# Whole F32 products for the first 256 tokens, and weights split after them, in a fused attention and expert kernel

## The chip, the cores and the metric

The kernel runs on one core of one Trainium2 chip. The metric is the device time of one execution in microseconds; of several executions the median is quoted. TensorE (PE) multiplies matrices, VectorE (DVE), ScalarE (ACT) and GpSimd (POOL) work elementwise, and SyncE (SP) issues the transfers. Each engine runs its own instructions in the order in which the program lists them and waits for others by semaphores.

## What is computed

Three layers stand in a row, over 4 sequences of 768 tokens with 8 heads of 48 columns (3072 tokens, 384 columns in all). The first is an attention with a complex decay per token and column (`a_re`, `a_im`, scaled to a magnitude of at most 0.999), the second an expert layer with a rational activation, the third a layer that changes only tokens whose score is positive.

```python
for t in range(S):
    ar, ai = (a_re_n[:, :, t, :, None], a_im_n[:, :, t, :, None])
    new_re = ar * S_re - ai * S_im
    new_im = ar * S_im + ai * S_re
    kv = np.einsum('bhd,bhe->bhde', k[:, :, t], v[:, :, t])
    S_re, S_im = (new_re + kv, new_im)
    y[:, :, t] = np.einsum('bhd,bhde->bhe', q[:, :, t], S_re)
...
x = np.ascontiguousarray(attn_out.transpose(0, 2, 1, 3)).reshape(B * S, H * D)
...
h = x @ w_in
h2 = h * h
h3 = h2 * h
P = a[0] + a[1] * h + a[2] * h2 + a[3] * h3
Q = 1.0 + np.abs(b[0]) * np.abs(h) + np.abs(b[1]) * h2
g = P / (Q + 1e-06)
return (g @ w_out).astype(np.float32)
...
do_compute = skip_score > 0
out = x.copy()
```

`w_in` is 384 x 2048 and `w_out` 2048 x 384; both arrive as 64-bit floats.

## The kernel before

**Tiling.** The 3072 tokens are worked through in 12 units of 256 (`u`), each of two chunks of 128. Of a unit, the attention part (`early`, `trig`, `cums`, `prods`, `chunk`) turns decays into sums of logarithms and angles, takes exponentials and sines, and makes scores and states by small products; `yevac` brings the result to SBUF and splits it into a rounded part `xh` and the rest `xl`. The expert part is 8 steps per unit (`step`, 96 in all). A step has two halves of G1 (line 819: 128 hidden columns x 256 tokens, three products of 384 input rows each), ten elementwise operations on a 128 x 512 tile (lines 366, 805 on ScalarE, 809 on VectorE), the split of their result into `gh` and `gl` (lines 848 and 851, GpSimd), and two halves of G2 (line 865), which add into the two `ob` banks.

**Split products.** The kernel multiplies in the type F32R. Each F32 operand stands as a rounded high part and the rest, the low part, and a product is three: high times high, high times low, low times high. Half a step of G1 is thus 9 matrix instructions of 256 columns and half a step of G2 is 6 of 384.

**Weights.** `weight_in` (8 transfers of 768 KB) and `weight_out` (16 of 384 KB) load the 64-bit words, and `weight` unpacks a piece of 384 columns by three VectorE operations (lines 395, 398, 405) and one scaling on ScalarE or GpSimd (366, 402), then rounds it on ScalarE (413) and subtracts on GpSimd (417). There are 32 such pieces. For room they unpack in buffers that have another use later: `weight_in` in `wk`, whose parts are the steps' `u` (`ub`) and `qa` (`qab`), `weight_out` in `xh1`, `xl1`, `x2b`, the last two parts of `wk`, `gh` and `gl`. Steps are listed behind all weights, and so a step's first elementwise operation, which writes `u` or `qa`, waits until all eight loads of `weight_in` have been unpacked and split.

**Order.** All work is listed as tasks in a `Plan`, with engines that may do it, a cost on each and what it reads and writes. `order` plays the list through by these costs: each engine takes the ready task with the lowest rank. A rank is a due time (`start`, `due`) or is counted back from the tasks that follow; `PP` holds the numbers that shape it. On TensorE a task in the other mode (`cols`: scores, values and updates of the state, which use parts of the array) is put back by `AF`. The result is written out in that order for every engine. Where the play leaves TensorE a gap between 5 us and `start(NP) + X1`, `filled` puts in products without a reader (lines 942, 946, 949); line 310 clears the banks at the start.

**After the steps** the output tiles are scaled, stored and scored (lines 366, 878, 883), and `flags` decides whether the rare paths run; they don't here.

## Time and profile before

| | us |
|---|---|
| median of 3 runs (653.58 to 654.98) | 653.9 |
| the profiled execution | 654.03 |
| its span, first to last instruction | 652.2 |
| mean share of the full TensorE clock granted | 0.994 |
| TensorE busy | 632.7 |
| ScalarE busy | 564.9 |
| VectorE busy | 534.3 |
| GpSimd busy | 426.5 |

The profile is of one execution; its span is 1.8 us shorter than the time that this execution took. "Busy" is time in which an engine works on at least one instruction; products overlap, so their durations add up to more than TensorE's busy time. A table by stretch gives for each engine the busy time inside it and the instructions in brackets, then the granted TensorE clock, the share of the time that the transfer engines are busy, and GB/s. A group of instructions is told by line, engine, operation and tiles, with its count, busy time and the mean duration of one in ns; behind the second bar stands the idle time before them. The view of one line gives minimum, median and maximum in ns and the first and last start. In the views by time a row gives start, duration and the instructions merged in it.

### The profile page before, as it was taken

How to read it: one execution, taken by the hardware profiler on the slowest of the kernel's cores; microseconds unless marked ns; L12 is line 12 of the kernel's file. 1: busy time of each engine (PE TensorE's matmuls, PEld its weight loads, DVE VectorE, ACT ScalarE, POOL GpSimd, SP SyncE). 2: the span in 40 equal slices, each digit the busy share in tenths (PEclk: the TensorE clock that was granted, in tenths of full speed). 3: DMA queues.
4: the chain of work that ended last, by engine and by line, in shares of the span. 5: the costliest groups of instructions: out<-in, count | busy, mean ns of one | idle time of the engine just before them, and what ended most of it. 6: DMA issues, size and time to landing. Idle time of an engine off the chain costs nothing.

```text
span 652.2 us, 15284 instructions
## 1 busy us (share of the span) xinstructions
PE 632.7 (97%) x5852; PEld 604.6 (93%) x5852; DVE 534.3 (82%) x859; ACT 564.9 (87%) x938; POOL 426.5 (65%) x425
## 2 busy tenths in 40 slices
PE   7899899999999999999999999999999999999994
PEld 6798889999999999999999999999999999999994
DVE  5999999898878798798798798798798797675772
ACT  6888899998999998997999997998999996976771
POOL 6688968876586686665576676665676766634442
PEclk9989999999999999999999999999999999999998
DMA  8728514113103023023112023023013020010000
GB/s 326 219 86 265 167 47 119 50 48 95 51 22 100 28 62 101 5 60 93 33 47 78 24 66 102 1 65 95 25 47 101 2 66 4 4 45 5 25 1 30
DMA packets 43698, 45.81 MB, mean 70 GB/s; under 512 B 19680, under 2 KB 40544, under 8 KB 43616
## 3 DMA queue, kind: packets, MB, share of 16 engines
q1 hardware_dynamic: 43616, 44.74, 22.7%
q8 instruction: 48, 0.79, 0.5%
q14 instruction: 34, 0.28, 0.1%
HBM read 38.73 MB, written 4.72 MB: 67 GB/s over the span
## 4 chain that ended last, share of the span: by engine, by line
PE 84%; DVE 6%; POOL 4%; ACT 2%; issue 1%; DMA 1%; SPq 0%; POOLq 0%; DVEq 0%
PE ob L865 30%; PE zb L819 30%; PE zb L671 6%; PE zb L691 5%; PE zb L714 4%; PE zb L737 3%; PE zb L716 2%; PE ob L949 2%; POOL kt L369 1%; DMA ar<-in_a_re_dram 1%; DVE zb L398 1%; DVE zb L395 1%; PE zb L593 1%; PE zb L620 1%; POOL gl L851 1%
## 5 line engine op out<-in xcount | busy, mean ns | idle before, releaser
L809 DVE SCALAR_TENSOR_TENSOR wk<-wk,cf,zb 128x512 f32<-128x512 f32 x192 | 141.8, 743 | 57.1 <-ACT zb L805 42.7
L819 PE MATMUL zb<-xh,wih 128*128 128x256 f32 x576 | 165.9, 288 | 0.2 <-DVE pT L696 0.2
L819 PE MATMUL zb<-xl,wih 128*128 128x256 f32 x576 | 162.3, 282 | 0.0
L819 PE MATMUL zb<-xh,wil 128*128 128x256 f32 x576 | 161.7, 281 | 0.0
L848 POOL TENSOR_SCALAR gh<-wk 128x512 fp32r<-128x512 f32 x96 | 64.2, 668 | 122.9 <-PE ob L865 95.9
L366 ACT ACTIVATE wk<-wk,cf 128x512 f32<-128x512 f32 x192 | 139.3, 727 | 1.3
L851 POOL TENSOR_TENSOR gl<-wk,gh 128x512 fp32r<-128x512 f32 x96 | 131.9, 1374 | 7.0
L865 PE MATMUL ob<-woh,gh 128*128 128x384 f32 x384 | 132.1, 344 | 0.0
L865 PE MATMUL ob<-woh,gl 128*128 128x384 f32 x384 | 129.7, 338 | 0.0
L865 PE MATMUL ob<-wol,gh 128*128 128x384 f32 x384 | 129.6, 338 | 0.0
L819 PEld LDWEIGHTS zb<-xh,wih 128*128 128x128 f32 x576 | 108.4, 188 | 3.7 <-issue 1.9
L819 PEld LDWEIGHTS zb<-xh,wil 128*128 128x128 f32 x576 | 108.6, 188 | 0.0
L819 PEld LDWEIGHTS zb<-xl,wih 128*128 128x128 f32 x576 | 108.3, 188 | 0.0
L805 ACT ACTIVATE wk<-zb 128x512 f32<-128x512 f32 x96 | 57.2, 596 | 34.2 <-PE zb L819 33.7
L865 PEld LDWEIGHTS ob<-woh,gh 128*128 128x128 f32 x384 | 72.1, 188 | 0.9 <-issue 0.7
L865 PEld LDWEIGHTS ob<-woh,gl 128*128 128x128 f32 x384 | 72.1, 188 | 0.3 <-POOL gl L851 0.3
L865 PEld LDWEIGHTS ob<-wol,gh 128*128 128x128 f32 x384 | 72.3, 188 | 0.0
L809 DVE SCALAR_TENSOR_TENSOR zb<-wk,cf,zb 128x512 f32<-128x512 f32 x96 | 71.8, 748 | 0.0
L809 DVE SCALAR_TENSOR_TENSOR wk<-wk,zb 128x512 f32<-128x512 f32 x96 | 65.4, 682 | 1.2
L805 ACT ACTIVATE wk<-zb,cf 128x512 f32<-128x512 f32 x96 | 66.0, 687 | 0.3 <-POOL gl L851 0.2
L805 ACT ACTIVATE zb<-wk 128x512 f32<-128x512 f32 x96 | 57.9, 603 | 9.0 <-DVE wk L809 7.9
L369 POOL TENSOR_TENSOR kt<-r,cs 128x768 f32<-128x768 f32 x21 | 45.9, 2193 | 4.1 <-DVE r L636 3.0
(194 smaller groups left out, 1349.6 us busy)
## 6 DMA issues: line engine op xcount, KB each, us to landing
wk<-in_moe_w_in_dram SPq DMA_DIRECT2D x8, 768.0 KB
ar<-in_a_re_dram SPq DMA_DIRECT2D x24, 192.0 KB
ai<-in_a_im_dram SPq DMA_DIRECT2D x24, 192.0 KB
kraw<-in_k_dram SPq DMA_DIRECT2D x24, 192.0 KB
qraw<-in_q_dram SPq DMA_DIRECT2D x24, 192.0 KB
vb<-in_v_dram SPq DMA_DIRECT2D x24, 192.0 KB
out_dram<-x2b SPq DMA_DIRECT2D x24, 192.0 KB
vo<-in_v_dram SPq DMA_DIRECT2D x48, 48.0 KB
```

The lines of the kernel that those rows point to most:

```text
L366: return ("ACT", cost, lambda: nc.scalar.activation(out=out, in_=in_, func=func, **kw))
L369: return (e, cost, lambda: eng[e].tensor_tensor(out=out, in0=in0, in1=in1, op=op), both)
L671: nc.tensor.transpose(z[0:112, i, :], src[:, 112 * h:112 * h + 112], ident)
L691: nc.tensor.matmul(z[o:o + 64, h, n:128], lhsT=K[:, h, n:n + 64], rhs=Q[:, h, n:128], start=True, stop=True)
L714: nc.tensor.matmul(dst, lhsT=vt, rhs=pT[hf][:, i, :], start=True, stop=first)
L737: nc.tensor.matmul(z[64 * o:64 * o + 64, h, :], lhsT=ktc[:, d:d + 64], rhs=vt[:, 48 * h:48 * h + 48], start=True, stop=True)
L805: return ("ACT", cost, lambda: nc.scalar.activation(out=h() if out is None else out, in_=h() if in_ is None else in_, func=func, **kw))
L809: return ("DVE", cost, lambda: nc.vector.scalar_tensor_tensor(out=h() if out is None else out, in0=in0, scalar=scalar, in1=h(), op0=op0, o ...
L819: nc.tensor.matmul(h()[:, i * 256:i * 256 + 256], lhsT=w[:, j, fs], rhs=x[:, j, :], start=(n == 0), stop=(n == 8))
L848: nc.gpsimd.tensor_scalar(out=g, in0=uu, scalar1=1.0, scalar2=1.0, op0=ALU.mult, op1=ALU.mult)
L851: eng[e].tensor_tensor(out=ghl("gl", s), in0=uu, in1=ghl("gh", s).bitcast(F32), op=ALU.subtract)
L865: nc.tensor.matmul(o, lhsT=a[:, sl], rhs=w[:, f, :], start=(f == 0 and n == 0), stop=(f == NF - 1 and n == 2))
```

## The change

**Products.** With `FU=1`, the unit of the first 256 tokens keeps its tokens, its weights and its activations in F32, and each product is taken once, in F32: half a step of G1 is 3 products instead of 9, of G2 2 instead of 6. It has no `xl`, `gh` and `gl`. The other eleven units are as before.

**Weights.** Each of the 32 pieces is loaded by a transfer of its own (384 KB) into one of 16 buffers (`stage`), unpacked there by the same four operations, and copied by a transfer within SBUF (`wcp`, 192 KB) to `wil` or `wol`. From there the first unit multiplies. When it has used a step's pieces, `split` rounds the two together to the high part, which takes a stage buffer, and subtracts in place: 16 roundings (ScalarE or GpSimd) and 16 subtractions (GpSimd or VectorE) of 768 columns instead of 32 of 384 each. The separate high tensors `wih` and `woh` are gone, and unpacking no longer uses the steps' buffers.

**Start.** The constants are made in two parts, `consts2` behind; some fills shrink. The coefficients (`coefs2`) come in three parts, the last one late (`C3` = 238). The loads of `a` for the first unit are four tasks; the two small loads of coefficients move to ScalarE's queue.

**Order.** The planner's costs are taken from traced durations, changes of mode on TensorE have a table of costs (`SW`), a task's rank has an offset by its name and unit (`RK`, some 190 numbers), and all numbers in `PP` are new, chosen by playing the list with random lengthenings of tasks. Among them: `AF` from 11.39 to 27.13, `E0`, which brings the due time of the first unit's tokens forward, from -30.164 to 53.32, `X1` from 24.0 to 34.5, and `DW`, how long ahead of its rank a load may be issued, from 980 to 16. Engines barred from tasks (`NO`) change too: `wlo`, `gl`, `tlo` may now also run on VectorE.

```diff
+    SW = ((0.0, 0.10, 0.12), (-0.08, 0.0, 0.09), (0.07, 0.06, 0.0))
...
+            t.rank = (t.due() if t.due else end - cost * (slack["2"] if t.late else slack[eng])) + PP["RK"].get(t.part, 0.0)
...
-                    if e == "PE" and t.cols != cols:
-                        cost += 0.1
-                        cols = t.cols
+                    if e == "PE":
+                        cost += self.SW[mode][t.kind]
+                        cols, mode = t.cols, t.kind
...
+        return two(n + str(u % 2), 768, F32 if u < FU else F32R).rearrange("p (j t) -> p j t", j=3)[:, :, sl]
...
-        nc.gpsimd.memset(state, 0.0)
...
+    def consts():
...
+    def consts2():
...
+    def coefs2(part):
...
+    NB = DM * (2 if wide else 1)
+    hiw = keep["hi"] = {"i": {}, "o": {}}
+    stages = {}
+
+    def stage(n):
+        if n not in stages:
+            stages[n] = keep["wp"].tile([128, NB], F32, tag=f"wh{n % (2 * NP)}", name=f"ws{n}")
+        return stages[n]
+
+    def weight_hi(m, p):
+        if p not in hiw[m]:
+            hiw[m][p] = keep["wp"].tile([128, 2, DM], F32R, tag=f"wh{p + (NP if m == 'o' else 0)}", name=f"w{m}{p}")
+        return hiw[m][p]
+
+    def weight(m, p, z, num):
 
...
+        pl.add(dma(lambda: [(stage(num).bitcast(I32), d_.bitcast(I32))], n=1), writes=keys + [h_], name=f"wld{m}{p}", xfer=0.34 * NB / DM * 2)
...
+        w = wil if m == "i" else wol
+        pl.add(dma(lambda: [(w[:, 2 * p + z, :].bitcast(F32), value())], n=1), reads=src, writes=[("wf",) + key], name="wcp", xfer=0.5)
...
+    def split(m, p):
+        ks = [(m, p, z) for z in range(2)]
+        w, h_, l_ = ([(n,) + k for k in ks] for n in ("wf", "wh", "wl"))
+        lo = (wil if m == "i" else wol)[:, 2 * p:2 * p + 2, :]
+        lf = lo.bitcast(F32)
+
+        def whi(e):
+            hi = weight_hi(m, p)
+            if e == "ACT":
+                nc.scalar.activation(out=hi, in_=lf, func=AF.Copy)
+            else:
+                nc.gpsimd.tensor_scalar(out=hi, in0=lf, scalar1=1.0, scalar2=1.0, op0=ALU.mult, op1=ALU.mult)
 
         def wlo(e):
+            eng[e].tensor_tensor(out=lo, in0=lf, in1=weight_hi(m, p).bitcast(F32), op=ALU.subtract)
+        pl.add([("ACT", 0.73, lambda: whi("ACT")), ("POOL", 0.85, lambda: whi("POOL"))], reads=w, writes=h_ + [("st", p + (NP if m == "o" else 0))], name="whi")
+        pl.add([("POOL", 1.85, lambda: wlo("POOL")), ("DVE", 0.87, lambda: wlo("DVE"), True)],
+               reads=h_, writes=w + l_, name="wlo")
+
+
+    def weights():
+        num = 0
+        for p in range(NP + 1):
+            for m, q_ in (("i", p), ("o", p - 1)):
+                if 0 <= q_ < NP:
+                    for z in range(2):
+                        weight(m, q_, z, num)
+                        num += 1
...
+        if u == 0:
+            for c in cc:
+                for i, n in enumerate(("ar", "ai")):
+                    pl.add(dma(lambda c=c, i=i: prs()[2 * cc.index(c) + i:2 * cc.index(c) + i + 1], n=1), writes=[n + str(c)],
+                           name="lda0", xfer=0.65, due=lambda c=c, i=i: -900.0 + 2 * i + c)
+            return
...
+        if u < FU:
+            return
...
+        whole = u < FU
+        xks = [(n, u % 2, c) for n in (("xh",) if whole else ("xh", "xl")) for c in range(2)]
...
+            X = xhl("xh", u)
+            wl = wil[:, 2 * p + i, :]
+            if whole:
+                pr = [(wl.bitcast(F32), X)]
+            else:
+                wh = weight_hi("i", p)[:, i, :]
+                pr = [(wh, X), (wh, xhl("xl", u)), (wl, X)]
             for j in range(3):
-                for w, x in ((wih, X), (wih, XL), (wil, X)):
-                    nc.tensor.matmul(h()[:, i * 256:i * 256 + 256], lhsT=w[:, j, fs], rhs=x[:, j, :],
-                                     start=(n == 0), stop=(n == 8))
+                for w, x in pr:
+                    nc.tensor.matmul(h()[:, i * 256:i * 256 + 256], lhsT=w[:, 128 * j:128 * j + 128], rhs=x[:, j, :],
+                                     start=(n == 0), stop=(n == 3 * len(pr) - 1))
                     n += 1
-        wks = [(n, "i", p, z) for n in ("wh", "wl") for z in range(2)]
+        wks = [(n, "i", p, z) for n in (("wf",) if whole else ("wh", "wl")) for z in range(2)]
         for i in range(2):
-            pl.add([("PE", 1.08, lambda i=i: g1(i))], reads=xks + wks + [("hd", s - NH) if i == 0 else hk + (0,)],
+            pl.add([("PE", 1.31 if whole else 1.08, lambda i=i: g1(i))], reads=xks + wks + [("hd", s - NH) if i == 0 else hk + (0,)],
                    writes=[hk + (i,)], due=at(0, i), bank=None if i else hk, name=f"G1_{s}_{i}")
...
+        if not whole:
...
+                wl = wol[:, f, :]
+                if whole:
+                    pr = [(uu, wl.bitcast(F32))]
+                else:
+                    g_h, g_l, wh = ghl("gh", s), ghl("gl", s), weight_hi("o", p)[:, i, :]
+                    pr = [(g_h, wh), (g_h, wl), (g_l, wh)]
                 sl = slice(i * 256 + t * 128, i * 256 + t * 128 + 128)
...
+            pl.add([("PE", 1.31 if whole else 1.055, lambda t=t: g2(t))], reads=([U] if whole else [GH, GL]) + wks, writes=[("o", t)],
...
+    pl.add([("ACT", 3.0, lead)], writes=["L", "cfr"], name="lnexp", due=lambda: -1e3, tail=-1.9)
+    pl.add([("POOL", 3.4, consts)], writes=["ys", "c0"], name="consts", due=lambda: -1e3)
+    pl.add([("POOL", 4.6, consts2)], reads=["c0"], writes=["c", "S", "ys", "qt"] + [(n, i) for n in ("v", "kt") for i in range(2)] +
+           [("dec", i) for i in range(ND)], name="consts2", due=lambda: PP["C2"])
...
+            weights()
...
+        if u == FU - 1:
+            for p in range(NP):
+                split("i", p)
+                split("o", p)
     out_ = pl.order(PP["SL"], PP["BI"], PP["DW"], PP["HO"], PP["TC"], PP["NO"])
```

## Rows read from the trace of the kernel before

**Rows 1.** The page's first part: busy time, share of the span and instructions by engine.
```profile
PE 632.7 (97%) x5852; PEld 604.6 (93%) x5852; DVE 534.3 (82%) x859; ACT 564.9 (87%) x938; POOL 426.5 (65%) x425
```
**Rows 2.** Table by stretch: busy PE, PEld, DVE, ACT, POOL; clock, transfers.
```profile
0.00:72.60 72.60, 65.22 (x570) 57.81 (x571) 62.61 (x131) 58.52 (x100) 57.53 (x86) 0.98 0.68 224
72.60:98.00 25.40, 23.51 (x266) 21.68 (x265) 25.14 (x39) 23.71 (x41) 18.00 (x17) 1.00 0.25 73
98.00:120.00 22.00, 22.00 (x173) 21.28 (x172) 21.61 (x35) 21.54 (x40) 17.93 (x19) 1.00 0.32 94
...
200.00:600.00 400.00, 399.22 (x3787) 385.09 (x3785) 328.11 (x504) 357.32 (x592) 255.59 (x234) 1.00 0.18 50
```
**Rows 3.** The same table for line 949 alone (fillers): busy PE and PEld.
```profile
0.00:72.60 72.60, 35.75 (x290) 34.75 (x290) 0.98 0.68 224
72.60:98.00 25.40, 5.34 (x35) 4.26 (x33) 1.00 0.25 73
```
**Rows 4.** Groups of instructions on TensorE: the other products without a reader.
```profile
L942 PE MATMUL ob<-trir 128*128 128x512 f32 x16 | 4.5, 439 | 0.0
L946 PE MATMUL ob<-trir 128*128 128x256 f32 x32 | 4.4, 291 | 0.0
...
L310 PE MATMUL zb<-trir 128*128 128x512 f32 x6 | 2.9, 656 | 2.3 <-POOL trir L283 2.3
```
**Rows 5.** View by time, 72 to 82 us: first expert products, first step operation.
```profile
72.61 0.36 PE L819 MATMUL zb<-xh,wih 128*128 128x256 f32 x1
...
80.44 2.56 POOL L417 TENSOR_TENSOR wil<-wk,wih 128x384 fp32r<-128x384 f32 x2
...
81.63 0.66 ACT L805 ACTIVATE wk<-zb,cf 128x512 f32<-128x512 f32 x1
```
**Rows 6.** The chain that ended last, in order of time, steady part.
```profile
173.56 1.08 PE zb L819 x9
...
178.85 2.52 POOL kt L369
...
192.37 1.27 PE zb L819 x9
...
323.41 2.52 POOL kt L369
...
587.55 1.26 PE zb L819 x9
```
**Rows 7.** View by time, TensorE, 57 to 60 us: F32 products by two passes each.
```profile
57.54 0.81 PE L596 MATMUL zb<-ai,trit 128*128 128x384 f32 x2
...
58.64 1.46 PE L623 MATMUL zb<-ta,trir 128*128 128x384 f32 x4
```
**Rows 8.** Unpacking and splitting of weights: a pair by time, two lines' durations.
```profile
14.01 1.01 DVE L395 TENSOR_SCALAR zb<-wk 128x384 int32<-128x384 int32 x2
...
L413 ACT ACTIVATE wih<-wk x16: 537/550/572, 17.8 to 80.3; 128x384 fp32r<-128x384 f32 x16
...
L417 POOL TENSOR_TENSOR wil<-wk,wih x16: 1011/1026/1766, 18.5 to 82.0; 128x384 fp32r<-128x384 f32 x16
```
**Rows 9.** Groups of instructions: a step's operation, 768-column ones, two inputs on VectorE.
```profile
L809 DVE SCALAR_TENSOR_TENSOR wk<-wk,cf,zb 128x512 f32<-128x512 f32 x192 | 141.8, 743 | 57.1 <-ACT zb L805 42.7 <-ACT wk L805 12.0
...
L585 DVE SCALAR_TENSOR_TENSOR ail<-ai,ta 128x384 fp32r<-128x384 f32 x20 | 20.2, 1011 | 1.4 <-ACT ta L580 1.3
...
L573 POOL TENSOR_TENSOR ar<-ta,tb 128x768 fp32r<-128x768 f32 x10 | 18.4, 1839 | 0.5
...
L490 ACT ACTIVATE tb<-ta 128x768 f32<-128x768 f32 x22 | 18.7, 848 | 0.0
```
**Rows 10.** First VectorE operation by time; longest wait of SyncE (total, times, longest).
```profile
3.28 0.55 DVE L499 TENSOR_SCALAR_CACHE_REDUCE ar<-ar 128x384 f32<-128x384 f32 x1 [3.28 <-DMA ar<-in_a_re_dram]
...
SPq L362 <- PE zb L737: 70.2, 9, 22.7
```
**Rows 11.** The chain again: the last products of the expert layer, G2 alone.
```profile
633.49 9.61 PE ob L865 x54
```

More of the change, by code (lines that the diff above doesn't have):

```diff
@@ L26 @@
 class Task:
-    __slots__ = ("opts", "deps", "succ", "rank", "bank", "free", "n", "name", "xfer", "only", "eng", "late", "tail", "due", "cols")
+    __slots__ = ("opts", "deps", "succ", "rank", "bank", "free", "n", "name", "xfer", "only", "eng", "late", "tail", "due", "cols", "part", "kind")
 class Plan:
+    SW = ((0.0, 0.10, 0.12), (-0.08, 0.0, 0.09), (0.07, 0.06, 0.0))
     LAT = {"PE": 0.2, "ACT": 0.2, "DVE": 0.12, "POOL": 0.12, "SP": 1.8}
@@ L42, in add @@
         t.only, t.eng, t.late, t.tail, t.cols = only, None, late, tail, cols
+        t.part = (name.split("_")[0].rstrip("0123456789") if name[:2] in ("G1", "G2", "cu", "rn", "re", "ex", "ld", "wl", "de", "cr") and name != "G1" else name, min(self.unit, 3))
+        if name[:2] in ("G1", "G2"):
+            t.part = (name[:2], t.part[1])
+        t.kind = 2 if cols else int(name == "xp")
         deps = set()
@@ L65, in order @@
             end = min((s.rank for s in t.succ), default=1e9) - self.LAT[eng] - t.xfer
-            t.rank = t.due() if t.due else end - cost * (slack["2"] if t.late else slack[eng])
+            t.rank = (t.due() if t.due else end - cost * (slack["2"] if t.late else slack[eng])) + PP["RK"].get(t.part, 0.0)
             t.eng = None
@@ L73, in order @@
         lock = {"DVE": 0.0, "POOL": 0.0}
-        cols = False
+        cols, mode = False, 0
         events = []
@@ L382, in weight, with words, value, upper @@
+    def weight(m, p, z, num):
         n = DM
-        h_, w_ = (tag + ("h",), ("wz", tag[0], part % 2))
+        slot = num % (2 * NP)
+        keys, key = [("st", slot)], (m, p, z)
+        h_, w_ = ("sh", slot), ("sw", slot)
         tk = ("wz",) + key
+        src = keys
+        d_ = (w_in[p][:, z * DM:(z + 1) * DM] if m == "i" else w_out[2 * p + z])
+        def words():
+            return stage(num).bitcast(I32).rearrange("p (n z) -> p z n", z=2)
+        def value():
+            return stage(num)[:, 0:DM]
+        def upper():
+            return words()[:, 1, :].bitcast(F32)
+        pl.add(dma(lambda: [(stage(num).bitcast(I32), d_.bitcast(I32))], n=1), writes=keys + [h_], name=f"wld{m}{p}", xfer=0.34 * NB / DM * 2)
@@ L407, in weight @@
                 reads=keys + [w_], writes=[h_], free=tk, name="wb3")
             src = keys + [h_]
-        else:
-            def t():
-                return shape(stg)
-            src = keys
-        pl.add([("ACT", 0.42, lambda: nc.scalar.activation(out=hi, in_=t(), func=AF.Copy))],
-               reads=src, writes=[("wh",) + key], name="whi")
-        def wlo(e):
-            eng[e].tensor_tensor(out=lo, in0=t(), in1=hi.bitcast(F32), op=ALU.subtract)
-        pl.add([("POOL", 1.02, lambda: wlo("POOL")), ("DVE", 0.47, lambda: wlo("DVE"), True)],
-               reads=[("wh",) + key] + src, writes=[("wl",) + key], name="wlo")
@@ L920, in main_part @@
                 load_v(ci + 2)
+        pl.unit = u + 1
         if nxt:
@@ L925, in main_part @@
             qrkr(u + 1)
+        pl.unit = u
         if u == 0:
-            for p in range(NP):
-                weight_in(p)
-            for f in range(NF):
-                weight_out(f)
+            weights()
         for p in range(NP):
             step(u * NP + p)
+        if u == FU - 1:
+            for p in range(NP):
+                split("i", p)
+                split("o", p)
     out_ = pl.order(PP["SL"], PP["BI"], PP["DW"], PP["HO"], PP["TC"], PP["NO"])
@@ L961, in exact_path @@
     BH = B * H
-    wih, wil, woh, wol = keep["wih"], keep["wil"], keep["woh"], keep["wol"]
+    wih, wil, woh, wol = keep["hi"]["i"], keep["wil"], keep["hi"]["o"], keep["wol"]
     ident, skip = keep["ident"], keep["skip"]
```

218 lines of the change are left out of this document (94 added, 124 removed).

## The prediction

> **What bounds the kernel now.** I read the totals first, then the stretches, then the chain. TensorE is busy for 632.7 of the 652.2 us span [rows 1], but not with the problem alone. While it has nothing to do, the kernel feeds it products that no one reads: 41.1 us from L949 [rows 3] and 4.5, 4.4 and 2.9 us from L942, L946 and L310 [rows 4], together 52.9 us. Real work is thus 632.7 - 52.9 = 579.8 us. Idle time is 652.2 - 632.7 = 19.5 us, of which 9.1 lie behind the last product, which ends at 633.49 + 9.61 = 643.1 [rows 11]; the other 10.4 and the 52.9 of fillers are 63.3 us in which TensorE did no real work before it was saturated. The ledger: 579.8 work + 63.3 start-up loss + 9.1 tail + 1.8 outside the span = 654.0 us, the profiled execution's own 654.03, 0.1 above the median of the runs.
>
> The loss lies in one place. After 98 us there are no fillers, and TensorE is busy for 22.00 of 22.00 and 399.22 of 400.00 us [rows 2]. From there on every microsecond is product time, and no other engine's relief is worth anything. Before that VectorE is the fullest engine: 62.6, 25.1 and 21.6 us of the stretches of 72.6, 25.4 and 22.0 us [rows 2]: 109.4 us in all, 0.937 of the time from its first instruction at 3.28 us [rows 10] to 120 us. ScalarE stands at 58.5, 23.7 and 21.5, GpSimd at 57.5, 18.0 and 17.9.
>
> The chain says why the start is so late. The first product of the expert layer runs at 72.61 us [rows 5]. Three steps' products run, then nothing follows: ScalarE touches the first of them at 81.63 us, while GpSimd splits the last two pieces of w_in (80.44 to 83.0) [rows 5]. That is the code: `weight_in` unpacks into the `wk` buffers that the steps need as `u` and `qa`, so no step can begin before all of w_in has gone through.
>
> **The change part by part.** *Whole products.* A 384-column F32 product runs as two passes; two passes take 0.81 and four 1.46 us from first start to last end, so a pass adds (1.46 - 0.81) / 2 = 0.325 us [rows 7] and one of 256 columns, scaled, 0.217. Half a step of G1 is 3 products, 6 x 0.217 = 1.30 us instead of 1.08; half of G2 is 2 products, 4 x 0.325 = 1.30 instead of 6 x 9.61 / 55 = 1.05 (54 instructions and the last one's tail) [rows 6, 11]. Eight steps take 8 x 4 x 1.30 = 41.6 us instead of 8 x 2 x (1.08 + 1.05) = 34.1: **+7.5 us** of TensorE work, certain, and free only where TensorE would have stood still.
>
> *Unpacking.* VectorE's three operations per piece stay: 96 at 0.505 (a pair takes 1.01) [rows 8] are 48.5 us. The rounding on ScalarE (32 x 0.55 = 17.6 us) and the subtraction on GpSimd (32 x at least 1.03 = 33 us) [rows 8] leave the path to the first products, as do GpSimd's low and high parts for eight steps. No step waits any more for all of w_in, since pieces have buffers of their own.
>
> *Copies.* 32 transfers within SBUF are added on SyncE, each between a piece's last unpacking operation and its product, and weights come in 32 loads instead of 24. No copy of this size is in the trace. The nearest row is the first load, issued in the first microsecond and used at 3.28 us [rows 10]; so 1 to 2.5 us each, at the upper end by the load's size. It delays a piece, not an engine, and is hidden while pieces are unpacked some microseconds ahead; if each step waited for it, it would cost up to 8 x 2.5 = 20 us. Behind each waiting copy SyncE's later loads are queued, and SyncE already waits a lot: 70.2 us in nine waits, up to 22.7, for one reason alone [rows 10].
>
> *The split behind.* 16 roundings and 16 subtractions of 768 columns return once a step of the first 256 tokens is through: at ScalarE's 0.85 us 13.6 us, at GpSimd's 1.84 us 29.4 us [rows 9]. ScalarE is busy 357.3 of 400 us in the steady part [rows 2], 43.1 of a unit's 48.2 us; spread over the first unit the split costs nothing, all in the second unit up to 43.1 + 13.6 - 48.2 = 8.5 us. I take 0, because the first unit has neither the high and low parts nor ScalarE's rounding.
> One row shows what GpSimd beside VectorE can do: a 384-column VectorE operation with two SBUF inputs takes 1.01 us on average at L585 [rows 9], twice the 0.505 of an unpacking one, which has at most one input there [rows 8]. The Trainium skill, page SBUF — State Buffer, section Who interferes with whom, says that such an instruction and a GpSimd one that reads SBUF exclude each other for a whole instruction, the later one waiting. By that rule the split's long subtractions would lengthen VectorE's list where it is the bound; the row agrees in kind. With some 6 such operations per unit in two units, each delayed by half of 1.84 us, an estimate of 11 us comes on top of my sum, against 0 beyond what the pace of 0.937 already holds.
>
> *Constants and coefficients.* What the first 256 tokens do not need is moved back. The constants shift a few of GpSimd's operations, and the loads of `a` get keys of their own: 1 to 2 us at the start, hidden under VectorE's list. Of the coefficients some 2 us stay early.
>
> *The new order.* In the steady part it can only save changes of TensorE's mode: G1 behind attention takes 1.27 instead of 1.08 us [rows 6], and I count 42 returns from attention's mode between 180 and 600 us, about 5 per unit; the first and the last of the marked kind, G1 in 1.27 us, stand in [rows 6]. All 11 units would give 11 x 5 x 0.19 = 10.5 us if none were left. The score for staying in a mode (`AF`) goes from 11 to 27; I take a quarter, 2.5 us, between 0 and 5. Tasks newly open to VectorE (`gl`, `tlo`, `wlo`) I cost at nothing in the steady part: it is busy for 39.5 us of a unit's 48.2 (below), so 8.7 us stand free, and what goes beyond them would lengthen every unit. Fillers may now stand until later (`X1`); one that is in the way of real work that comes earlier than the planner played delays it by one filler's 0.23 us, a few times at most. The tail stays.
>
> *The start-up loss.* VectorE is what remains as its bound. A unit takes (323.41 - 178.85) / 3 = 48.2 us [rows 6], in which VectorE is busy 328.1 / 400 x 48.2 = 39.5 us [rows 2]; eight steps of four operations at 0.743 [rows 9] are 23.8 of it, attention 15.7. Until the first 256 tokens are through, VectorE needs 48.5 + 23.8 + two attentions 31.4 + 2 = 105.7 us, at a pace of 0.937 from 3.3 us: until 116 us. TensorE's real work by then: the 41.6 us and two attentions of 48.2 - 34.1 = 14.1 us, 69.8. That is a loss of 46 us, plus the last step's series of six operations at about 0.74, 4.5 us, with little else to run: **50.8 us** instead of 63.3. The sum: 579.8 + 7.5 - 2.5 + 50.8 + 9.1 + 1.8 = **646.5 us**. Note what carries it: VectorE's bound does not fall, the order within it does. Before, VectorE unpacked late weights while the steps were locked out.
>
> **The rivals.** *The surcharge is paid and the start is not shortened* (slower). Mechanism: a piece reaches its product only after VectorE, an in-order SyncE queue and a copy; if waiting copies hold back loads of later pieces and of `a`, the first unit runs at the copies' pace and the loss stays at 63.3. Price: 579.8 + 7.5 - 2.5 + 63.3 + 10.9 = 659.0 us. It decides from a loss of 63.3 - 5.0 = 58.3 us on. For it: SyncE's long waits [rows 10]; against: the copies are listed in the order in which VectorE ends the pieces. Chance 0.15.
> *Only the lock-out goes.* The first product still comes at 72.6 us, where 35.8 + 11.8 us of fillers and 7.4 idle are 55.0 already lost [rows 2 to 4], but from there the steps flow: 579.8 + 7.5 - 2.5 + 55.0 + 10.9 = 650.7 us. This is also the case in which the change brings only half of what it says. For it: attention and weights share VectorE, and buffers of their own let even more pieces be unpacked ahead of it; against: the offset that sets the due time of the first tokens (`E0`) now calls for them earlier. Chance 0.12.
> *The split comes due in the second unit* and finds ScalarE full: +8.5 us, 655.0. For it: ScalarE's 43.1 of 48.2 us; against: GpSimd has room (255.6 of 400) [rows 2] for the subtractions, and the pieces come free one by one. Chance 0.13.
> *VectorE's list runs denser* (0.98 as in 98 to 120 us), no lag, and half of the mode changes go: loss 3.3 + 105.7 / 0.98 - 69.8 = 41.4, 579.8 + 7.5 - 5 + 41.4 + 10.9 = 634.6. Chance 0.20.
>
> **How the numbers follow.** The forecast has 0.40, a loss of 46 to 55 us, 642 to 651. A measurement here can tell about 0.2%, 1.3 us, from no change. Faster: 0.39 of the forecast, 0.20 of the dense list, 0.09 of the lock-out case and 0.04 of the late split, 0.72. Slower: 0.14 of the surcharge and 0.04 of the late split, 0.18. Same: 0.10. The range reaches from near the dense list (637) to near the surcharge (658), leaving about 0.1 out on each side.
>
> **What would show it.** Right: the first F32 product well before 72 us, ScalarE's first step operation within 2 us of it, fillers of 30 to 40 us instead of 52.9, no filler or gap after about 120 us, real TensorE work near 585 us, VectorE over 0.93 until then. Wrong: a G1 half far from 1.30 us; TensorE gaps between 120 and 170 us that wait for L413's successor (late split); products waiting for a DMA of `wil` or `wol` (surcharge); VectorE well below 0.93 in the first 110 us, which would mean that something else bounds the start; a unit period above 48.2 us.

## The result: 660.7 us, one per cent slower

The changed kernel takes 660.65 us (median of 4 executions, 660.36 to 661.2) where the kernel before takes 653.74 in the same comparison: a ratio of 1.0105, 95% interval 1.0087 to 1.0123. I had forecast 646.5, with a range of 637 to 658, so the time lies outside it, on the other side of no change. The profiled execution took 660.53 us, its span is 658.8.

The page of the changed kernel: busy time by engine, and the shares of the chain that ended last.

```profile
PE 635.8 (97%) x5698; PEld 594.4 (90%) x5698; DVE 560.1 (85%) x883; ACT 570.7 (87%) x940; POOL 348.6 (53%) x343
...
PE 60%; ACT 16%; DVE 14%; issue 3%; DMA 3%; POOL 1%; SPq 1%; ACTq 0%; DVEq 0%; POOLq 0%
```

TensorE is busy 3.1 us longer than before [rows 1] although fewer products have no reader. Those are four groups on TensorE (count, then busy time and mean ns):

```profile
L998 PE MATMUL ob<-ident 128*128 128x128 f32 x248 | 31.5, 284 | 0.0
...
L991 PE MATMUL ob<-trir 128*128 128x512 f32 x16 | 4.7, 455 | 0.0
L995 PE MATMUL ob<-trir 128*128 128x256 f32 x32 | 4.0, 283 | 0.0
...
L319 PE MATMUL zb<-trir 128*128 128x512 f32 x6 | 2.9, 656 | 1.5 <-POOL nedge L290 1.5
```

They sum to 43.1 us, 9.8 less than the 52.9 before [rows 3, 4]; real work is 635.8 - 43.1 = 592.7 us, 12.9 more. The table by stretch, as in [rows 2], shows where TensorE stands idle:

```profile
0.00:72.60 72.60, 68.21 (x549) 59.18 (x550) 61.95 (x132) 56.20 (x90) 30.87 (x68) 1.00 0.82 268
72.60:98.00 25.40, 23.49 (x178) 19.74 (x176) 25.13 (x39) 23.37 (x39) 16.01 (x15) 0.93 0.44 143
98.00:120.00 22.00, 22.00 (x198) 16.72 (x198) 21.69 (x41) 18.72 (x33) 17.95 (x14) 1.00 0.46 139
120.00:200.00 80.00, 76.17 (x692) 70.43 (x690) 69.50 (x102) 75.78 (x125) 51.56 (x39) 1.00 0.20 56
200.00:600.00 400.00, 397.74 (x3762) 380.48 (x3762) 343.22 (x507) 362.26 (x602) 222.15 (x196) 1.00 0.18 51
```

VectorE is as full as before up to 120 us (108.8 against 109.4 us), and TensorE now has holes behind 120 us: 3.8 us up to 200, 2.3 behind it, where before had 0.8 from 200 on.

I cut the time at the first G1 product of units 1, 3 and 11. This is added up from the start and end of every product (where two products overlap, the later one counts from the end of the earlier; "fill" is all four groups without a reader, line 310 and its successor 319 among them, so it comes out smaller than their busy times added up):

| stretch | before: length (work / fill / gap) | after: length (work / fill / gap) | change |
|---|---|---|---|
| start to unit 1 | 118.9 (60.3 / 49.4 / 9.3) | 116.6 (69.4 / 40.9 / 6.3) | -2.3 |
| unit 1 to unit 3 | 96.5 (96.0 / 0 / 0.5) | 97.4 (93.6 / 0 / 3.8) | +0.9 |
| unit 3 to unit 11 | 384.9 (384.2 / 0 / 0.8) | 391.3 (389.1 / 0 / 2.3) | +6.4 |
| unit 11 to its last product's end | 42.7 | 42.7 | 0 |
| from there to the end of the span | 9.1 | 10.8 | +1.7 |

The two rows that bound the longest stretch, from the view of TensorE by time:

```profile
214.05 0.28 PE L852 MATMUL zb<-xh,wi 128*128 128x256 f32 x1
...
605.36 0.28 PE L852 MATMUL zb<-xh,wi 128*128 128x256 f32 x1
```

So the change gains 2.3 us where it was made, and loses 6.4 us in eight units whose products, weights and elementwise operations it does not touch; only their order and the choice of engines are others. That is the question for the chip.

### The profile page after: what moved, and what is told of

It is laid out like the page before. It is cut to its first block, busy times and chain, and to the rows that moved or that the text cites. A ratio compares the mean times of both kernels' runs of the same rounds, so it can differ in the third digit from the quotient of the medians.

```text
span 658.8 us, 15052 instructions
## 1 busy us (share of the span) xinstructions
PE 635.8 (97%) x5698; PEld 594.4 (90%) x5698; DVE 560.1 (85%) x883; ACT 570.7 (87%) x940; POOL 348.6 (53%) x343
## 4 chain that ended last, share of the span: by engine, by line
PE 60%; ACT 16%; DVE 14%; issue 3%; DMA 3%; POOL 1%; SPq 1%; ACTq 0%; DVEq 0%; POOLq 0%
PE ob L904 21%; PE zb L852 20%; PE zb L696 5%; PE zb L716 4%; PE zb L739 4%; ACT wk L832 3%; DVE wk L836 3%; PE zb L741 2%; PE zb L762 2%; ACT tb L515 1%; ACT wk L375 1%; DVE ai L518 1%; ACT L551 1%; DVE zb L836 1%; ACT L366 1%
## 5 line engine op out<-in xcount | busy, mean ns | idle before, releaser
L852 PE MATMUL zb<-xh,wi 128*128 128x256 f32 x528 | 152.9, 290 | 0.3 <-ACT qT L702 0.2
L852 PE MATMUL zb<-xl,wi 128*128 128x256 f32 x528 | 148.7, 282 | 0.0
L904 PE MATMUL ob<-wo,gh 128*128 128x384 f32 x352 | 120.9, 344 | 1.6 <-DVE x2b L917 1.6
L904 PE MATMUL ob<-wo,gl 128*128 128x384 f32 x352 | 119.0, 338 | 0.6 <-DVE gl L884 0.6
L904 PE MATMUL ob<-wol,gh 128*128 128x384 f32 x352 | 118.9, 338 | 0.0
L852 PEld LDWEIGHTS zb<-xh,wi 128*128 128x128 f32 x528 | 99.3, 188 | 3.6 <-issue 1.4
L852 PEld LDWEIGHTS zb<-xl,wi 128*128 128x128 f32 x528 | 99.4, 188 | 0.3
L884 POOL TENSOR_TENSOR gl<-wk,gh 128x512 fp32r<-128x512 f32 x62 | 87.0, 1404 | 22.5 <-DVE gh L879 17.4
L904 PEld LDWEIGHTS ob<-wo,gh 128*128 128x128 f32 x352 | 66.1, 188 | 2.9 <-DVE x2b L917 1.9
L904 PEld LDWEIGHTS ob<-wo,gl 128*128 128x128 f32 x352 | 66.1, 188 | 0.9 <-DVE gl L884 0.9
L378 POOL TENSOR_TENSOR qt<-r,cs 128x768 f32<-128x768 f32 x19 | 40.3, 2123 | 12.4 <-ACT cs L552 7.7
```

Of the source, the lines that this page charges most:

```text
L378: return (e, cost, lambda: eng[e].tensor_tensor(out=out, in0=in0, in1=in1, op=op), both)
L852: nc.tensor.matmul(h()[:, i * 256:i * 256 + 256], lhsT=w[:, 128 * j:128 * j + 128], rhs=x[:, j, :], start=(n == 0), stop=(n == 3 * len(pr) ...
L884: eng[e].tensor_tensor(out=ghl("gl", s), in0=uu, in1=ghl("gh", s).bitcast(F32), op=ALU.subtract)
L904: nc.tensor.matmul(o, lhsT=a[:, sl], rhs=w, start=(f == 0 and n == 0), stop=(f == NF - 1 and n == len(pr) - 1))
```

## Experiments

Two theories. **Graph:** the added work (F32 surcharge, copies, split, the room that they take) costs more than forecast. **Order:** the new order costs the time, and the graph with another order would be quicker. Kernels called "ordered" have their tasks in a fixed list for each engine in place of the planner's ranks, so that single tasks can be placed; this edit is common to them:

```diff
-        ready = {e: [] for e in engines}
+        by = {t.key: t for t in self.tasks}
+        seq = {e: [by[k] for k in v.split(",")] for e, v in json.loads(zlib.decompress(base64.b85decode(ORDER))).items()}
```

### The changed graph in the order of before

The tasks that both kernels have stand on the engines and, as nearly as their dependences allow, in the order of before. Copies follow the unpacking, the split follows each step.

```diff
+                k, r = k.rsplit(" ", 1)
+                eng[k], rank[k] = e, float(r)
+        seq = {e: sorted((t for t in self.tasks if eng[t.key] == e), key=lambda t: (rank[t.key], t.n)) for e in tab}
```

> The changed kernel with its buffers, its F32 first unit and its late split, but every instruction that both kernels have goes to the engine and stands in the order that the kernel before gave it; the copies and the late split are put in where their data are ready. Theory 'order': the changed kernel's loss of 6.5 us between the first G1 of unit 3 and that of unit 11 (391.4 us against 384.9) is its order, so this run takes 385 us (at most 386.5) for that stretch, and 650 to 658 us in all. Rival 'graph': the new buffers or the F32 start slow the steady part whatever the order, so the stretch stays at 390 to 392 us and the whole at 658 us or more.

Measured: 663.34 us (662.22 to 664.56), ratio 1.0127 (1.0099 to 1.0155). The whole says little, because this order starts late: unit 1 at 122.7 us. The stretch from unit 3 to unit 11 takes 387.6 us, and unit by unit the periods are those of before within 0.3 us in seven of the eight, and the other is 2.2 us longer (50.8 against 48.6), where the replayed order departs. With the same graph as after, 3.7 of the 6.4 us are thus gone, and 2.7 stay. At 387.6 us the stretch lies between the two forecasts (at most 386.5, or 390 to 392). Where the order is the same, the graph does not lengthen a unit; the expected total was wrong, since I had not seen that this order would hold the start back.

### Surcharge, copies and split, each by itself

One F32 product more in each half of G1 of the first unit adds 6.9 us to TensorE's work there:

```diff
+            if whole:
+                nc.tensor.matmul(h()[:, i * 256:i * 256 + 256], lhsT=wl[:, 0:128].bitcast(F32), rhs=X[:, 0, :],
+                                 start=True, stop=True)
```

> The changed kernel with one more F32 product (128x256, 0.43 us as a third of a half of G1) ahead of each of the 16 halves of G1 of the first unit, overwritten by the half itself: 6.9 us more of TensorE work in the stretch from 52 to 110 us. Theory 'VectorE sets the start': TensorE has fillers and gaps there until 100 us and only the four halves behind that are on the path, so the whole grows by 0 to 2 us, to 661 to 662.5. Rival 'the surcharge is paid in full', as the prediction's ledger has it: 667 to 668.

Measured: 663.31 us, ratio 1.0143 (1.0113 to 1.0172), 0.8 us above the range of the first theory and far below the rival's. Unit 1 starts at 118.7 instead of 116.6, and the stretch behind is 391.3 as in after. Of 6.9 us of added work 2.1 arrive there: TensorE is not what bounds most of the start.

VectorE's first unpacking operation issued twice adds 14.8 us to VectorE's list:

```diff
+            def first():
+                for _ in range(2):
+                    nc.vector.tensor_scalar(
+                        out=bits(), in0=words()[:, 0, :], scalar1=29, scalar2=None, op0=ALU.logical_shift_right)
+            pl.add([("DVE", 0.47, first)],
```

> The changed kernel in its own order, but the first of the three VectorE instructions that unpack a piece of the weights is done twice (the second writes the same bits again): 32 x 0.46 us from start to start = 14.8 us more on VectorE, all of it ahead of the first G1 of unit 1. Theory 'VectorE sets the start', by which the prediction put that product at 116 us: it moves from 116.6 to 128 to 132 us, and the whole grows by 11 to 15 us, to 671 to 676. Rival 'something else sets it' (the copies on SyncE's queue, the F32 work of TensorE): below 122 us, and the whole below 666.

Measured: 675.88 us, ratio 1.033 (1.029 to 1.0369). Unit 1 starts at 131.4 us, 14.8 later; the stretch from unit 3 to 11 stays 391.3. All of the dose arrives: VectorE's list sets the start, as the prediction had it.

The split's subtraction over 48 of its 768 columns only (the low parts of the rest are left wrong, and the rare paths then run at the end, so that only the trace up to the last product counts):

```diff
+            c = slice(0, 48)
+            eng[e].tensor_tensor(out=lo[:, :, c], in0=lf[:, :, c], in1=weight_hi(m, p).bitcast(F32)[:, :, c], op=ALU.subtract)
```

> The changed kernel in its own order, but the 16 subtractions that make the low parts of the weights behind the first unit take 48 of each 768 columns only; the low parts of the rest are left out. About 27 us of GpSimd's work between 62 and 150 us falls away. Theory 'hidden', as predicted: 659.5 to 661. Rival 'split due in the second unit': TensorE's gaps from 130 to 200 us (3.6 us) come from it, so 656.5 to 658.

Measured: 893.59 us as a whole, with the rare paths. The last expert product ends at 646.8 instead of 648.0 us. Unit 1 starts 1.0 us earlier, and between units 1 and 3 the gaps are 3.78 us as in after (3.83). The split's subtractions cost some 1.2 us in this order, and the gaps behind 120 us are not theirs; its 16 roundings stayed, and no run takes them away alone.

### What VectorE was newly given

After has 26 of its 88 `gl` on VectorE by the trace (another number in the expectation is a miscount of mine), before none. In an ordered kernel they go to GpSimd, all else staying:

> The changed kernel in its own order, but the 34 subtractions for the low part of the activations that VectorE does go to GpSimd, at the same place in the order. Theory 'shared list': VectorE's 34 (0.69 us where nothing is in the way, 2.2 us where GpSimd is at work) are what TensorE's waits of the steady part come from, so the whole falls to 656 to 659 us. Rival 'helper': the same work takes 1.3 us on GpSimd and comes later, the second products wait for it, and the whole grows to 662 to 666 us.

Measured: 660.71 us, ratio 1.0095 (1.0061 to 1.013); unit 3 to unit 11 392.2 us. That theory falls: `gl` on VectorE is not what lengthens the units. After also has 16 of its 88 `gh` on VectorE and 8 on ScalarE, where before has all on GpSimd; no run moves these back alone, but the third order below has 19 `gh` and 24 `gl` on VectorE and no gap.

The largest waits of TensorE behind unit 1's start in after (sum, times, longest) name VectorE:

```profile
PE ob L904 <- DVE x2b L917: 1.6, 1, 1.6
PE zb L739 <- DVE pT L721: 1.5, 1, 1.5
PE zb L696 <- DVE kt L378: 1.0, 1, 1.0
PE ob L904 <- DVE gl L884: 0.6, 1, 0.6
PE zb L619 <- DVE ail L610: 0.4, 1, 0.4
```

The second of them by time, VectorE and GpSimd:

```profile
187.01 1.00 POOL L578 TENSOR_TENSOR ai<-ai,cs 1x384 f32<-1x384 f32 x1
187.52 2.54 DVE L378 TENSOR_TENSOR qt<-r,cs 128x768 f32<-128x768 f32 x1
187.98 1.27 POOL L884 TENSOR_TENSOR gl<-wk,gh 128x512 fp32r<-128x512 f32 x1
189.99 0.68 DVE L721 TENSOR_TENSOR pT<-zb,mask 128x512 int32<-128x512 int32 x1
```

A rotation of q (two SBUF inputs, 0.95 us where nothing disturbs it) lasts 2.54 us and ends 0.8 us after GpSimd's two operations are through at 189.25; the mask `pT` behind it is late, and TensorE waits. So I took the rotations that stood on VectorE behind the first unit to GpSimd, in after's order:

> The changed kernel's own order with the rotations of q and k that stood on VectorE (16 behind the first unit) moved to GpSimd. Theory 'VectorE operations lengthened beside GpSimd cause the gaps': the gaps from the fourth to the last unit's start fall from 2.26 us to under 1.2 and the stretch from 391.3 to 389 or 390; the whole 658 to 659.5. Rival 'the order is too tight there, whichever engine has the rotations': a rotation takes 1.85 us on GpSimd, the gaps stay or grow, the stretch is 391 to 394 and the whole 660 to 663.

Measured: 661.52 us (660.04 to 662.0), ratio 1.0116 (1.0087 to 1.0144). Unit 1 starts earlier, at 113.9, and the stretch from unit 3 to 11 grows to 395.5 us with 5.1 us of gaps. Its waits in that stretch:

```profile
PE zb L666 <- POOL kt L348: 2.6, 6, 0.7
PE zb L686 <- ACT qT L672: 1.1, 3, 0.4
PE zb L822 <- ACT qT L672: 0.6, 1, 0.6
```

There the waits move to GpSimd's rotations and to what follows them; between units 1 and 3 the gaps fall from 3.8 to 2.4 us. In sum the gaps behind unit 1 grow from 6.1 to 7.5 us. That is the rival's side, with a stretch even above its 391 to 394 us: this order leaves too little time between a rotation and its product on either engine. What the lengthened VectorE operations cost by themselves is not shown by it, since the run also loads GpSimd.

### TensorE's changes of mode

The products of attention that use parts of the array (scores, values, updates) are entered 38 times between units 3 and 11 in before and 48 times in after. An ordered kernel regroups TensorE's list alone, to 41 entries:

> The changed kernel with the other engines' order untouched, but TensorE's own order regrouped so that from unit 3's first G1 to unit 11's the change into the 64-wide products is made 41 times and not 48 (38 in the kernel before). Theory 'mode changes': at about 0.2 us for each way in and out the stretch falls from 391.4 by 1.2 to 1.6 us, and the whole to 659. Rival 'waits': what stands in the order between is moved too, new waits for ScalarE and VectorE take the gain, and the stretch stays at 391 or above, the whole at 660 to 663.

Measured: 658.86 us (658.13 to 660.07), ratio 1.0081 (1.0054 to 1.0107); the stretch takes 388.2 us, 3.1 less: 3.4 less product time (385.7 instead of 389.1) and 0.3 more gap. Its bounds:

```profile
214.83 0.28 PE L822 MATMUL zb<-xh,wi 128*128 128x256 f32 x1
...
603.06 0.28 PE L822 MATMUL zb<-xh,wi 128*128 128x256 f32 x1
```

Seven entries fewer, with what was moved for them, take back half of the 6.4 us, twice what I expected. The gaps (2.5 us) stay, and 1.8 us of the 3.1 reach the whole.

### Both graphs, ordered with the same care

If the order is at fault, the changed graph with a better one must win, and against before's graph that was ordered in the same way, not only against before as it stands. Both were ordered by moving single tasks to other places or engines and keeping what ended earlier, with durations from the traces that were lengthened at random. First one order of each:

> The changed kernel's instructions all kept, but each engine's order and the choice of engine searched further by single moves, with each order scored under random lengthenings of the traced durations. Ways into the 64-wide products between unit 3 and unit 11: 37. Theory 'the order is the loss': the waits of the steady part (4.2 us), its mode changes (2.2), the gaps from 130 to 200 us (3.3) go, and the start gains some: 644 to 652 us, faster than the kernel before. Rival 'the F32 first unit and the late split are the loss': at best the 654 to 656 that the order of before gives, so 654 or more.

> The kernel before with its own instructions, its order searched in the same way and as long. It tells what the F32 first unit and the late split are worth once both orders are alike in care. Theory 'the graph gains at the start': this run stays 3 to 9 us above the reordered changed kernel, at 647 to 655 us. Rival 'the graph gains nothing': it lands within 1 us of it or below.

then two more of each, from other starting orders or searched further:

> The changed graph again, its order found by the same search by single moves from another starting order; some 212 of 2851 tasks sit on another engine than in the first searched order. Theory 'the order is what the change lost by': this one too comes out well below the change's own order, 643 to 650 us, with the second unit's start near 111 us and the stretch from the fourth to the last unit's start at 385 to 389 us. Rival 'the first searched order was a lucky one': 652 to 662 us.

> The changed graph, a third search from a third starting order. Theory 'the order is what the change lost by': 643 to 650 us, within some 3 us of the other two searched orders, so that the spread of searched orders is smaller than their distance from the change's own order (15.6 us). Rival 'lucky first order': a spread over 8 us.

> The graph of before, a second search. If the graph itself is worth what the first pair of searched orders differs by (645.1 against 651.8 us), this comes out at 650 to 654 us. If that distance was chance among orders, it can come out at 643 to 648 us.

> The graph of before, the first searched order searched on further until 201 of 2856 tasks had changed their engine. If the graph is worth 3 to 7 us at equal care: 648 to 654 us, and all orders of before's graph stay above all orders of the changed graph. If not, the two groups overlap.

Measured, the six searched orders beside the two originals (work and gaps between units 3 and 11):

| order | median us | ratio to before | unit 1 starts | unit 3 to 11 | entries | work | gap | last product ends |
|---|---|---|---|---|---|---|---|---|
| before | 653.74 | 1 | 118.9 | 384.9 | 38 | 384.2 | 0.8 | 643.1 |
| before's graph, 1st | 651.75 | 0.9955 to 0.9987 | 110.5 | 385.8 | 31 | 382.3 | 3.5 | 637.8 |
| before's graph, 2nd | 657.15 | 1.0021 to 1.0055 | 122.8 | 385.8 | 32 | 384.8 | 1.0 | 644.1 |
| before's graph, continued | 654.0 | 0.9984 to 1.001 | 114.7 | 382.1 | 30 | 381.9 | 0.2 | 638.6 |
| after | 660.65 | 1.0087 to 1.0123 | 116.6 | 391.3 | 48 | 389.1 | 2.3 | 648.0 |
| changed graph, 1st | 645.09 | 0.9824 to 0.9938 | 111.0 | 387.3 | 37 | 386.6 | 0.7 | 634.9 |
| changed graph, 2nd | 651.12 | 0.9804 to 0.9957 | 117.4 | 383.8 | 35 | 383.5 | 0.3 | 640.1 |
| changed graph, 3rd | 643.31 | 0.9805 to 0.9843 | 110.6 | 384.8 | 37 | 384.8 | 0.0 | 629.6 |

The changed graph in its third order runs at 643.31 us (642.3 to 644.17), 1.8% faster than before and 2.6% faster than the changed kernel: the best version of this study. Its chain and two stretches of its table:

```profile
PE 88%; DVE 3%; DMA 3%; ACT 2%; SPq 2%; issue 1%; POOL 0%; DVEq 0%; ACTq 0%; POOLq 0%
...
120.00:200.00 80.00, 80.00 (x755) 75.55 (x754) 72.99 (x116) 74.30 (x121) 52.61 (x43) 1.00 0.17 49
200.00:600.00 400.00, 400.00 (x3788) 386.98 (x3787) 347.87 (x568) 352.31 (x580) 196.29 (x170) 1.00 0.18 52
```

TensorE is busy for all of the 480 us, with VectorE fuller than in after (347.9 against 343.2 us of 400). So neither VectorE's share nor the graph prevents a gapless order. The three orders of the changed graph average 646.5 us, the three of before's graph 654.3: 7.8 us for the graph, 5.3 of them at the end of the last product (634.9 against 640.1), with a spread among orders of one graph of 5 to 8 us. Three against three is little, and one of before's three only continues another: the runs point to a gain of the graph, but do not settle it. The slowest searched order of the changed graph and the fastest of before's are 0.6 us apart, and with the two originals counted in the groups overlap. That the order is what the changed kernel loses by is shown without this: the same graph takes 9.5 to 17.3 us less in three other orders.

Of the expectations, the first pair came as forecast. The second search of the changed graph (651.1) lies just above its 643 to 650 us, and the three orders spread over 7.8 us, where I had expected some 3. The second search of before's graph (657.2) lies above both of its forecasts, and the continued one (654.0) within its range, but slower than the order that it continued.

### One operation of 10 us

The changed graph's second order took 651 to 652 us in three of its executions and 642.6 in one. Its profile is of a long one. VectorE, GpSimd and TensorE by time, then its table for 110 to 120 us:

```profile
106.72 10.03 DVE L580 SCALAR_TENSOR_TENSOR ail<-ai,ta 128x384 fp32r<-128x384 f32 x1
...
104.93 0.99 POOL L548 TENSOR_TENSOR ai<-ai,cs 1x384 f32<-1x384 f32 x1
105.89 1.82 POOL L426 TENSOR_TENSOR wol<-wol,wo 128x768 fp32r<-128x768 f32 x1
107.67 0.99 POOL L769 TENSOR_TENSOR xl<-ys,xh 128x384 fp32r<-128x384 f32 x1
108.64 0.82 POOL L423 TENSOR_SCALAR wo<-wol 128x768 fp32r<-128x768 f32 x1
109.44 0.82 POOL L423 TENSOR_SCALAR wi<-wil 128x768 fp32r<-128x768 f32 x1
110.23 0.82 POOL L423 TENSOR_SCALAR wo<-wol 128x768 fp32r<-128x768 f32 x1
111.03 5.30 POOL L426 TENSOR_TENSOR wil<-wil,wi 128x768 fp32r<-128x768 f32 x3
...
116.80 0.69 PE L589 MATMUL zb<-ail,trir 128*128 128x384 f32 x1 [6.23 <-DVE ail L580]
...
110.00:120.00 10.00, 3.77 (x14) 2.81 (x13) 10.00 (x7) 2.09 (x4) 6.33 (x5) 0.68 0.10 36
```

A VectorE operation that elsewhere takes about 0.55 us begins 0.8 us behind a GpSimd one (105.89) and ends 0.4 us after the eighth in a row, counted from that one. TensorE waits 6.2 us for it, and during that idle time its granted clock falls from 1.00 to 0.50, the lower of its two levels of 1.2 and 2.4 GHz, from 113.7 to 120.5 us (0.68 over that slice); so the first products of unit 1 run at the lower level too. For the short execution the record has a mean granted clock of 0.996, for the three long ones 0.987 to 0.989: it had less of the low clock. Whether it lacked the long operation, no trace shows. I broke the row by giving three roundings (L423) to ScalarE, at the place where it stood idle:

```diff
-POOL: ... whi 3, whi 10, whi 1, wlo 8 ...
+POOL: ... wlo 8 ...
-ACT: ... a5 6, a1 7 ...
+ACT: ... a5 6, whi 3, whi 10, whi 1, a1 7 ...
```

> The second searched order of the changed graph with three of the split's roundings moved from GpSimd to ScalarE, so that GpSimd's row of eight instructions from 105.9 to 116.3 us has a pause where it must wait for ScalarE. Theory 'a VectorE operation with two SBUF inputs waits until GpSimd pauses': the low part of the angles (L580) lasts under 3 us instead of 10.03, TensorE's wait of 6.2 us for it goes, the second unit starts at 109 to 112 us instead of 117.4, the whole takes 641 to 645 us instead of 651.1. Rival 'VectorE was late there for another reason': L580 still ends near 116 us and the whole stays at 650 to 652.

Measured: 649.61 us (645.2 to 652.93), ratio 0.9939 (0.9913 to 0.9965). By time:

```profile
105.95 3.92 DVE L580 SCALAR_TENSOR_TENSOR ail<-ai,ta 128x384 fp32r<-128x384 f32 x1
...
106.69 0.99 POOL L769 TENSOR_TENSOR xl<-ys,xh 128x384 fp32r<-128x384 f32 x1
107.65 1.80 POOL L426 TENSOR_TENSOR wil<-wil,wi 128x768 fp32r<-128x768 f32 x1
113.20 3.61 POOL L426 TENSOR_TENSOR wil<-wil,wi 128x768 fp32r<-128x768 f32 x2 [3.75 <-ACT wi L421]
```

GpSimd's row now ends at 109.45, and VectorE's operation 0.4 us later, at 109.87; TensorE's wait for it is gone, and unit 1 starts at 110.5 instead of 117.4. At its place it is shown that the operation waits for GpSimd to pause, and that this wait held unit 1 back; why it did not come in sooner is not shown (see the end). It still took 3.92 us, where I had expected under 3. As a forecast of the whole the expectation failed, since only 2.3 of the 6.9 us reach the last product (637.8 against 640.1): units 1 to 3 take 98.7 us instead of 96.2, and the stretch behind 385.9 instead of 383.8. The roundings now stand in ScalarE's list; that this is the reason was not tried.

## Why the prediction was wrong, point by point

**The start was right.** VectorE's list was to last until 116 us: unit 1 starts at 116.6. The loss up to there was to be 50.8 us: fillers of 43.1 and 6.3 of gaps are 49.4. The dose on VectorE arrived in full, that on TensorE by a third, so the bound is the one that I named. The first F32 product was to come well before 72 us, and came at 52.05; ScalarE took up its halves at 56.13, 4.1 us behind the first product instead of the 2 that I gave, with six operations of attention in between. VectorE's share of 0.93 held (108.8 us from 3.3 to 120), and so did its work: 105.4 us of it up to unit 1, where I had added up 105.7. That the loss agrees as well is partly luck: for the 4.5 us of the last step's series no idle time shows, since TensorE is busy for all 22.00 us from 98 to 120 and the last group of fillers starts at 92.11; the rest of the 49.4 is a little less real work by then and the overlaps of products. And the fillers are 43.1 us, not the 30 to 40 that I gave as a sign.

**The surcharge was right.** Up to unit 3 TensorE works 163.0 us instead of 156.3, +6.7 against +7.5. A half of G1 and one of G2, from the chain of after:

```profile
87.06 1.29 PE zb L852 x6
88.36 1.29 PE ob L904 x4
```

Both stand at 1.29 us, where I had 1.30.

**The order's term had the wrong sign.** I took -2.5 us for changes of mode, between 0 and -5, because the score for staying in a mode had gone up from 11 to 27. The trace shows 48 entries instead of 38, and 4.9 us more product time in the same products: 7.4 us of the miss. The regrouped order ties 3.4 of the 4.9 to the entries and what moves with them; for the rest the tie is the correlation at the end. Real work came to 592.7 us instead of 585, and a unit to 48.9 us (391.3 / 8), above the 48.2 that I had named as a sign of being wrong. I read a number of the planner as if it were its result; which of the other numbers that were changed with it outweighed it was not tried. Nothing in the profile of before could show that order, so the honest bounds were some 5 us to both sides; with +5 in place of -2.5 the upper end of the range, 658, would have stood near 665.

**"No gap behind 120 us" was wrong.** I took the units behind the start as saturated by themselves. They were saturated in before's order [rows 2]. In after 6.1 us of gaps stand there. They are not those of the split's subtractions (which cost 1.2 us), not those of `gl` on VectorE, and moving the rotations to GpSimd leaves 7.5 us of them. What takes them away is another order of the same graph (0.0 to 0.7 us of gaps behind unit 3 in three orders). So it is the placing; which of the many placements matter most I did not separate.

**The end** takes 10.8 instead of 9.1 us behind the last product, +1.7. Over the runs it lies between 9 and 12.5 us with the same instructions in it; its cause was not tried and stays open.

**The sum of it:** -0.8 (surcharge) + 7.4 (entries) - 1.4 (start) + 6.1 (gaps) + 1.7 (end) = 13.0 of the 14.1 us between 646.5 and 660.6; the other 1.1 is about the difference between the two ways of counting busy time.

**The rivals.** "The surcharge is paid and the start is not shortened" gives 659.0 us, near what was measured, and is wrong all the same: the loss at the start fell to 49.4 us and no copy is among the waits of TensorE up to 116 us. A time that fits does not confirm its mechanism. "Only the lock-out goes" is out, since the first product came at 52.05 us and not at 72.6. "VectorE's list runs denser" is not seen either: even in the third order of the changed graph, which starts unit 1 at 110.6, VectorE is busy for 100.6 us from 3.3 us to there, a share of 0.94; it has less work ahead of unit 1 than in after (105.4 us), not a denser list. "The split comes due in the second unit" is half right in another order: there it did not fill ScalarE but stood in a row on GpSimd and cost 6.9 us at unit 1's start. The Trainium skill, page SBUF — State Buffer, section Who interferes with whom, has the rule for such a pair of instructions, and the prediction carried it beside its sum at an estimate of 11 us, against 0 taken. In after the value taken was the nearer (1.2 us); in the other order the rule was, though the wait there was for eight instructions and not for one. As for the chances, 0.72 for faster was a chance for the graph (7.8 us by three orders each) and not for the one order that came with it: I gave the order no rival of its own.

## What to carry to other kernels

When a change replaces an order as well as the work, forecast the two apart, and give the order bounds on both sides however well the work is understood: here the changed work seems to gain some 8 us, and the order that came with it takes 14 us more than the average of three that were searched. Compare graphs only with orders that were made with the same care, several of each, since orders of one graph spread by 5 to 8 us. And read the stretch that the change does not touch first: a difference there points to the order, and to the engines and the room that the change took.

## What the runs showed of the hardware

**Entering the mode of partial products.** Over the eleven kernels whose stretch from unit 3 to 11 was measured so (the eight of the table, and those with before's order, with regrouped products and with the rotations moved), product time rises by 0.39 us for each entry (a straight line through 30 to 48 entries and 381.9 to 390.3 us, correlation 0.92). That is twice the 0.19 us which the prediction took from the first products behind attention alone [rows 6]. It is a correlation, not a price: the orders differ in more than their entries. The regrouped order alone gives 3.4 us for 7 entries, 0.48 each, and the order with the rotations moved has 1.2 us more product time than after at the same 48.

**When VectorE waits for a row of GpSimd instructions.** Mostly it does not. In the traces of all sixteen kernels, 257 VectorE operations with two SBUF inputs start during a GpSimd instruction that reads SBUF and is followed by the next without a pause. Of these, 235 come in as soon as that one instruction is through, and it is GpSimd's next one that is held up. So in after, where GpSimd's rotations take 1.82 us at the least:

```profile
135.19 2.09 POOL L378 TENSOR_TENSOR qt<-r,cs 128x768 f32<-128x768 f32 x1 [3.66 <-ACT cs L552]
135.61 2.22 DVE L884 TENSOR_TENSOR gl<-wk,gh 128x512 fp32r<-128x512 f32 x1
137.24 2.29 POOL L378 TENSOR_TENSOR kt<-r,cs 128x768 f32<-128x768 f32 x1
```

Another 11 end before that instruction does. The last 11 waited for more than one: 2.54 us beside two, 3.92 beside three, 10.03 beside eight, each ending 0.4 to 0.8 us after GpSimd's last. In ten of these eleven, the GpSimd instruction that was running, or the one right before it, is its operation on a single partition (`ai<-ai,cs`, 1x384, in the rows shown); among the other 246 that is so once. What makes these rows different was not tried. A long row on GpSimd can thus have a price of its own, even where GpSimd has time to spare: here 6.9 us at unit 1's start.
